# A fifth buffer for q and k rows, and a new written-out order for all engines, in a one-core transformer block

## The chip, the cores and the metric

The kernel runs on one core of one Trainium2 chip. A core has five engines that are used here, each with its own queue of instructions: PE (TensorE: matrix products, into eight PSUM banks), DVE (VectorE), ACT (ScalarE), POOL (GpSimd) and SP (SyncE, which only issues transfers here). Transfers (DMAs) are issued from the queues of SP and POOL, and one from ACT's. The metric is the device time of one execution in microseconds (us); lower is better.

## The reference, cut to what matters

The input `x` is 2048 tokens of 448 features, in bf16. Everything starts from the layer-normalised `xn`:

```python
x = A_x
xn = _layernorm(x, axis=-1)
s = _A_ref(xn, A_wqkv, A_wo)                          # attention: 16 heads of 28, each token sees
                                                      # itself and 7 earlier ones, two apart
g = _silu(_B_ref(xn, B_w1, B_b1, B_w2, B_b2))         # MLP: gelu(xn @ w1 + b1) @ w2 + b2, 448 -> 1792 -> 448
return x + s * g
```

`_A_ref` makes q, k and v from `xn @ wqkv`, takes a softmax over the eight logits of a token and a head, weighs v with it and multiplies by `wo`.

## The kernel before, in words

**Tiles.** The tokens are reordered so that even ones come before odd ones; a window two apart then has neighbouring rows. They make 16 token tiles of 128 rows (t = 0 to 15) and four chunks of 512 (c = 0 to 3). The work of one token tile is: statistics (`stats`, L327), `rstd` (`rstds`, L338), normalisation (`norm`, L361), a transpose to `xnT` (on PE for tiles 0 to 3, by a DMA that SP issues, `dma_T` L274, for the others), the products for its q rows, k rows and v rows (`qk_rows` L448, `vproj` L471), and the copies of these out of PSUM. q and k rows go to a buffer `qk_tok` (L456 to L464), from which one DMA per tile writes them transposed to `qkT`; a buffer may be written again only when that DMA has landed (the third dependency in L461). Before the change there are four such buffers, and tile t uses buffer t mod 4. v rows are copied by DMAs that POOL issues (`values`, L485) into 128-row windows for the attention.

**MLP.** `ff1` (L506) makes 14 tiles of the hidden layer for each chunk, ACT applies the gelu; `ff2` (L530) makes one token tile of the result in two halves of seven products each; a token tile's result passes DVE, ACT (a tanh, or a silu for the last chunk) and DVE.

**Attention.** Nine blocks of 228 or 224 tokens (b = 0 to 8). `scores` (L660) is 64 small products into four banks, ACT takes the exponential, DVE multiplies by a mask, `values_sum` (L665) is 64 small products into two banks, DVE divides (`output_of`, L631: transpose, reciprocal, transpose, multiply), `final` (L673) multiplies by `wo`, then by the MLP's result, adds x and stores.

**Pairs and hops.** The products with 448 rows of contraction (q, k, v, ff1) run in pairs (`pair`, L401): a first part A of eight products, where the two jobs of a pair use the two halves of PE's rows at the same time, and a second part B of six with the halves exchanged. Between A and B stands a hop (L412): a nop on POOL or SP that waits for the end of A, and for which B waits. A hop stands in that engine's queue like any instruction: what is ahead of it in the queue delays B.

**The order.** There are 938 tasks, numbered in the order in which the code adds them. The string `ORDER` (L17) lists all of them; a word is an engine's letter (P = PE, V = DVE, A = ACT, G = POOL, S = SP, D = a transfer's landing) and a task's number. Each engine's instructions are issued in just this order, and PSUM banks and ring buffers are taken and given back in it (`emit`, L94). Tasks that may run on two engines (copies out of PSUM, hops) run on the one whose letter stands there.

The words that are spoken of below:

| words | task |
|---|---|
| P132 to P138 | first products of tiles 0 and 1, six batches and a last one |
| P149, P151; P128, P129 | q, k of tile 2, parts A and B; PE transposes of tile 3 |
| P190, V191 | transpose of the bias b1 on PE (L768), its copy |
| P308 A, P310 B; P313, P315; P318, P320; P323, P325; P333, P335; P338, P340 | ff1 of chunk 0, hidden tiles 0-1; 2-3; 4-5; 6-7; 10-11; 12-13 |
| P227, P215, P234, P208 | part A of q, k of tiles 6, 5, 7, 4 (P229, P217, P236, P210: part B) |
| A218, V219 or A219; A237, A238; A211, A212 | copies of q and k rows of tile 5; tile 7; tile 4 |
| S141, S146, S154, S161 | DMA that turns q and k rows of tile 0, 1, 2, 3 |
| S202, S206, S198, S194 | DMA that turns xn of tile 6, 7, 5, 4 |
| G99, G98, G307, G298 | rstd of tiles 6-7; 4-5; 12-15; 8-11 (L349) |
| G100, G102, G104 | building the three masks (L726) |
| G309, G314, G334, G529, G539 | hops before P310, P315, P335, P530, P540 |
| P691, P772 | scores of block 0; values of block 4 |
| G399, G403, G405 | POOL's DMAs of v rows of tile 8 for block 4 |

Of the kernel before, what the change touches and what calls it, by code (L numbers as in the profile page):

```python
# [11 lines left out]
ACT = mybir.ActivationFunctionType  # L12
# [3 lines left out]

ORDER = """  # L17
D0 V1 G17 S34 D35 A36 D37 V15 V16 P2 V22 S38 D39 V23 G50 V24 G51 D52 V25 V26 P3 V27 V28 S44 D45 V29 V30 G31 V18 V19
G32 P4 V20 G33 V21 S40 D41 P5 A53 S42 D43 P6 G100 S46 D47 P7 V60 P8 S48 D49 P9 V61 S76 D77 G102 V64 A62 P10 S78 D79
V63 P11 P12 V106 P13 S80 D81 P14 V107 P108 V65 S82 D83 P109 G104 A66 V110 S86 D87 V67 A111 D112 P132 V113 S88 D89  # L20
V114 P115 P116 S90 D91 V68 P136 A117 A118 D119 P133 V69 V72 A70 P134 V71 V120 P135 V121 V73 V101 P122 A74 A54 P123
V103 P137 V75 V124 D125 P138 V126 V127 P149 V105 A139 V140 A144 P128 G150 P129 V145 S141 D142 P151 A130 D131 V143
P190 A152 P308 V153 G168 D169 A148 V94 G170 D171 P313 S154 D155 G309 V95 G172 D173 V84 P310 G314 G174 D175 V85 P315
V191 V96 G178 D179 A311 P156 G176 D177 V97 V92 A312 G99 P163 V93 A316 P318 A317 G157 G164 V200 G98 P158 V201 V204
S202 D203 V205 P165 A159 V160 G319 P320 A166 V167 S206 D207 P323 G180 D181 A321 V196 V197 G182 D183 V192 P328 A322
S198 D199 V193 G324 G184 D185 P325 G329 G186 D187 S194 S146 D147 D195 P330 G188 D189 A326 P227 G246 D247 A327 S161
D162 P234 A331 G228 G252 D253 P229 A332 G235 G280 D281 S272 D273 P236 S274 D275 V231 A230 P215 S276 D277 P208 G216
S232 D233 P217 G209 P210 A218 V219 S278 D279 P333 A211 V212 S220 D221 P338 G334 P335 G339 A237 V238 P340 A336 S213
D214 P528 A337 P533 A341 G529 A342 P530 G534 P535 A531 V296 P538 A532 V297 V290 S239 D240 P543 A536 G539 V291 V294
A537 P540 V295 G544 V305 P545 A541 V306 V299 P548 A542 V300 V303 P553 A546 G549 V304 V301 A547 P550 G554 V302 V292  # L30
G307 P555 A551 V293 P558 A552 P222 A556 V431 G559 G298 V432 G223 P560 V427 A557 S433 D434 V419 P241 A561 G242 P224
A562 A225 A55 G248 D249 G282 D283 V428 V420 G284 D285 P243 A245 G286 D287 G288 D289 V423 G250 D251 V424 P691 A694
S429 D430 V226 V355 V356 S425 D426 S421 D422 V244 P568 P569 P508 A692 V570 G254 D255 A571 V572 V693 P513 P514 A698
V699 P727 P518 V515 V343 V351 V344 A696 G256 D257 P509 A516 V517 A732 G258 D259 V695 A728 V697 P700 G260 D261 S357
V347 D358 G262 D263 V348 A734 V735 V352 S345 D346 V510 A511 A730 V701 S349 D350 G264 D265 V702 V703 V705 P519 V520
V706 V707 S353 D354 V708 P523 V704 G266 D267 P524 P709 A712 V713 A716 V512 A714 V715 V731 G268 D269 V525 P359 S360
A710 P366 S367 P361 A362 P368 A370 P385 V363 G270 D271 V717 S386 P378 G379 P387 P380 S364 D365 V369 V711 P718 S371
D372 A388 G397 D398 P853 A389 V382 P573 A381 S383 D384 V719 P745 V723 V724 S390 D391 V733 V854 A748 A752 V855 V725
A750 P563 P574 A521 V720 V749 V721 V722 P564 V522 A746 V726 P863 V729 S856 D857 A526 P858 P736 V565 P454 V527 V864
G401 D402 V859 V860 G455 V741 P461 V575 P456 A457 V865 V737 G462 A458 V747 P449 V742 V743 V738 S866 D867 S459 D460  # L40
V744 P463 A464 A465 P468 S466 D467 G450 P451 V453 P442 G469 V751 P470 A471 V739 P435 S443 P444 V740 A446 A445 A566
G436 P437 A439 V753 V472 P754 V438 S440 D441 P868 P763 V452 V759 A766 V760 V869 P873 V870 V761 V567 V874 A768 A770
V762 A764 S447 D448 P578 P579 V580 A576 V577 V755 P781 A786 P373 A782 A788 V756 S871 D872 S861 D862 P583 S584 G374
P375 V376 G407 D408 P585 A784 A56 A377 P588 A581 S589 V757 G409 D410 V758 G411 D412 V767 V765 P593 P392 S594 A587
P590 P595 A586 G415 D416 V769 G399 D400 V771 V875 S393 A591 G403 D404 G473 P603 S876 D877 P394 S604 A597 P608 V395
A596 G405 D406 G413 D414 G417 D418 V789 G474 D475 P605 V787 A396 P772 G476 D477 G478 D479 G480 D481 A592 G482 D483
A606 V785 G484 D485 G486 D487 P598 V582 A607 S609 V773 V774 G488 D489 P613 V775 G490 D491 V783 S599 P600 G492 D493
V776 G494 D495 A602 A601 S614 P615 A616 P610 V777 V778 V779 V780 A612 P790 V795 P618 V791 A617 V796 A611 A57 P799
A800 V797 V798 G496 D497 P888 V889 P619 V620 P878 A804 V890 P883 A802 G498 D499 P817 S891 D892 V879 A818 V803 G500
D501 A621 A806 V880 V807 A822 P628 V805 G502 D503 V801 V884 P623 V792 V793 A820 V622 G504 D505 A824 P629 V630 V794  # L50
P808 V809 V810 V811 P624 G506 D507 P835 P893 A842 A840 V813 P633 P634 A838 V812 A836 A58 V635 A636 P648 V894 V895
S896 D897 P638 V814 V637 A631 P643 G639 S881 D882 V815 V816 V821 P640 A642 A641 V843 V625 V885 S649 P650 S644 A652
P645 P653 V823 A626 V819 A647 V841 P658 A646 S659 G654 V632 A651 P655 A657 A656 V825 V627 P660 S886 D887 A661 P826
V831 V837 P668 V832 V833 A662 G669 P663 G664 P670 V834 P665 A667 A671 A666 V839 P844 V849 P903 V904 V905 S906 D907
P908 V909 V910 V850 A672 A59 V827 P681 S911 D912 P682 V828 V829 V830 P673 V845 V851 P898 P674 P913 V899 V675 V900
A676 V846 V683 V847 P918 V848 A684 V852 V914 V915 S916 D917 P677 P678 V679 A680 V919 S901 D902 V920 S921 D922 P923
V924 P685 P686 V925 S926 D927 A687 P928 V929 V930 P688 P689 P933 A690 V934 V935 S931 D932 S936 D937
"""


# [58 lines left out]
def kernel(  # L119
# [13 lines left out]
    P = 128  # L133
    S, D, H, DH, F = A_x.shape[1], 448, 16, 28, 1792
# [16 lines left out]
    for v in range(9):  # L151
        n = NW - 1 if v == 4 else NW
        q = 4 * NW * v - 4 * (v > 4)
# [17 lines left out]
    def sb(name, shape, dt=BF16):  # L171
        return const.tile(shape, dt, name=name)
# [27 lines left out]
    def ring(name, n, shape, dt=BF16):  # L200
        return _Pool([sb(f"{name}{i}", shape, dt) for i in range(n)])
# [13 lines left out]
    p_g.bufs = p_g.bufs + late_g  # L215
    p_h = ring("h", 28, [P, CH])
    p_v = ring("v", 6, [P, H, 32])
    qk_tok = [sb(f"qk_tok{i}", [P, 2, H, 32]) for i in range(4)]
    p_b = _Pool([psum.tile([P, 512], F32, name=f"bank{i}") for i in range(8)])

    plan = _Plan()

    def buf(pool, owner, i=0):
        return pool.bufs[owner.slots[pool][i]]

    def copy(e, o, i):
        if e == "ACT":
            nc.scalar.copy(o, i)  # L228
        else:
            nc.vector.tensor_copy(o, i)  # L230


    def memset(eng, ap, v):
        def fn(_):
            getattr(nc, eng).memset(ap, v)
        return fn

    warm = p_h.bufs[-1]
    t_on = plan.add("DMA", lambda _: None, ())
# [12 lines left out]
                                base=0, pattern=[[-1, P]], channel_multiplier=1)  # L252
    t_ident = plan.add("POOL", mk_ident, [t_on])

    t_qz = [plan.add("DVE", memset("vector", q[:, :, :, DH:], 0.0), [t_on]) for q in qk_tok]
    t_vw = [plan.add("DVE", memset("vector", v[:, :, DH:], 1.0), [t_on]) for v in v_tok[:9]]
    t_row0 = plan.add("POOL", memset("gpsimd", row0[:], 0.0), [t_on])
    t_row0 = plan.add("POOL", memset("gpsimd", row0[:1, :], 1.0), [t_row0])
# [132 lines left out]
    def half_rows(half):  # L391
        return slice(64 * half, 64 * half + 64) if half < 2 else slice(0, P)
# [53 lines left out]
    t_row, t_qk = [[] for _ in range(NT)], {}  # L446

    def qk_rows(t, which):  # L448
        cs = slice(t * P, (t + 1) * P)

        def part(ps, kt, half, start, stop):
            r = half_rows(half)
            w = w_in[r, kt, which * D:(which + 1) * D] if kt < 3 else w_in3[r, 0, :]
            return nc.tensor.matmul(ps[:, :D], xnT[r, kt, cs], w, start=start, stop=stop)  # L454

        def evac(a, own, i):  # L456
            b = qk_tok[t % len(qk_tok)]

            def fn(k):
                copy(k.on, b[:, which, :, :DH], buf(p_b, own, i)[:, :D].rearrange("p (h c) -> p h c", h=H))  # L460
            t_row[t].append(plan.add(("ACT", "DVE"), fn, [a, t_qz[t % len(qk_tok)], t_qk.get(t - len(qk_tok))], give=((p_b, own, i),)))  # L461
            if len(t_row[t]) == 2:
                t_qk[t] = dma_T(qkT[:, :, :, cs].rearrange("p w g c -> p (w g) c"), lambda: b[:].rearrange("p w h c -> p (w h c)"),
                                t_row[t], None)  # L464
        return _Job(D, part, [t_xT[t]] + t_w[0] + t_w[1] + t_w[2], evac, (), t_w[3])
# [368 lines left out]
```

## Time and profile before

| what | value |
|---|---|
| three runs | 155.38, 156.09 and 156.47 us; median 156.09 |
| the profiled execution: its own time | 155.29 us |
| its span, first to last instruction | 153.6 us, so 1.69 us lie around it |
| PE busy | 148.3 us (97% of the span), 2200 products |
| DVE / ACT / POOL busy | 111.9 / 85.1 / 43.6 us (73 / 55 / 28%) |
| share of the chain that ended last | PE 83%, DMA 5%, DVE 4%, POOL 3%, SP's queue 2% |
| DMA that turns q and k rows, issue to landing | 3.1 / 4.9 / 8.1 us (least, median, most of 16) |
| the same for xn | median 3.3 us (12 of them) |

A profile line such as "L546 PE MATMUL ... x238 | 45.1, 342" means: 238 instructions of line 546, 45.1 us busy in all, 342 ns for one. Products are pipelined, so one lasts longer than the distance to the next; the cost of a product on PE's path is that distance. In the chain by time a line gives the start, the length and the work, in us. In the list of waits a line gives the waiting engine and what it waited for, then the total, the number of times and the longest.

### The profile page before, as it was taken

To read this page: it belongs to the slowest core of one execution; us is meant where nothing else is said; L and a number is where in the kernel's file an instruction comes from. 1 tells how busy PE (TensorE), PEld (TensorE's weight loads), DVE (VectorE), ACT (ScalarE), POOL (GpSimd) and SP (SyncE) were. 2 spreads that over 40 slices of the span, in tenths; PEclk is the share of its full clock that TensorE was granted. 3 is DMA by queue.
4 is the path that set the end of the run, shared out by engine and by line. 5 is a ranking of instruction groups with operands and counts; after the bars stand their busy time and mean duration, and the time that the engine had idled before them with its cause. 6 is when DMAs were issued, how large, how long until landed. Compare 5 with 4: busy or idle time off the path is not lost.

```text
span 153.6 us, 5265 instructions
## 1 busy us (share of the span) xinstructions
PE 148.3 (97%) x2200; PEld 80.9 (53%) x2200; DVE 111.9 (73%) x280; ACT 85.1 (55%) x158; POOL 43.6 (28%) x95
## 2 busy tenths in 40 slices
PE   6899999999999999999999999999999999999992
PEld 2444445578775555555554554455455444455561
DVE  4998541459262699969897997389859497797973
ACT  3474665368886350737043759739670859580320
POOL 7854865000359116020000004499500000000000
PEclk9999999999999999999999999999999999999999
DMA  5999998999987635079217370323300010010022
GB/s 149 326 276 324 126 187 168 226 343 257 165 112 150 111 73 103 4 147 131 63 34 137 74 132 19 98 71 86 81 30 4 4 60 30 4 47 17 0 89 65
DMA packets 33576, 17.36 MB, mean 113 GB/s; under 512 B 25203, under 2 KB 32387, under 8 KB 33552
## 3 DMA queue, kind: packets, MB, share of 16 engines
q1 hardware_dynamic: 31472, 14.03, 44.5%
q0 software_dynamic: 1936, 2.88, 7.9%
q8 instruction: 17, 0.28, 0.8%
q10 hardware_dynamic: 144, 0.11, 0.2%
q14 instruction: 7, 0.06, 0.1%
HBM read 7.06 MB, written 1.84 MB: 58 GB/s over the span
## 4 chain that ended last, share of the span: by engine, by line
PE 83%; DMA 5%; DVE 4%; POOL 3%; SPq 2%; issue 1%; ACT 1%; POOLq 0%; ACTq 0%
PE bank L546 28%; PE bank L512 22%; PE bank L454 10%; PE bank L681 8%; PE bank L477 6%; PE bank L627 4%; PE bank L595 4%; DMA qkT<-qk_tok 3%; POOL v L270 2%; DMA x_sb<-in_A_x_dram 2%; SPq L276 2%; DVE xn L363 1%; DVE st L329 1%; PE bank L378 1%; DVE xn L368 0%
## 5 line engine op out<-in xcount | busy, mean ns | idle before, releaser
L546 PE MATMUL bank<-w,h 128*128 128x448 bf16 (+2 forms) x238 | 45.1, 342 | 0.0
L512 PE MATMUL bank<-xnT,w 64*128 64x512 bf16 x392 | 44.7, 376 | 0.3 <-ACT qk_tok L228 0.3
L270 POOL DMA_DIRECT2D v<-v_tok x52 | 27.3, 532 | 48.4 <-DVE v_tok L230 27.1
L516 ACT ACTIVATE h<-bank,b 128x512 bf16<-128x512 f32 x56 | 34.2, 692 | 12.3 <-PE bank L512 12.2
L512 PEld LDWEIGHTS <-w 64*128 64x128 bf16 x392 | 23.1, 94 | 18.7 <-issue 1.0
L546 PEld LDWEIGHTS <-h 128*128 128x128 bf16 x238 | 22.1, 98 | 18.9
L605 ACT ACTIVATE E<-bank 128x456 bf16<-128x456 f32 (+1 forms) x36 | 17.2, 551 | 14.8 <-PE bank L595 14.8
L454 PE MATMUL bank<-w_in,xnT 64*128 64x448 bf16 (+1 forms) x212 | 24.0, 350 | 0.2 <-DVE xnT L230 0.2
L228 ACT CAST qk_tok<-bank 128x448 bf16<-128x448 f32 x20 | 9.9, 534 | 13.7 <-PE bank L454 9.8
L454 PEld LDWEIGHTS <-xnT 64*128 64x128 bf16 (+1 forms) x212 | 10.4, 94 | 10.1 <-issue 0.4
L561 DVE TENSOR_TENSOR y<-bank,b 128x448 f32<-128x448 f32 x15 | 9.2, 612 | 7.6 <-PE bank L546 7.6
L681 PE MATMUL bank<-wo,oT 128*128 128x448 bf16 (+2 forms) x68 | 14.3, 342 | 0.0
L637 DVE STREAM_TRANSPOSE dt<-bank 128x480 f32<-128x480 f32 (+1 forms) x18 | 11.8, 662 | 2.9 <-PE bank L627 1.7
L477 PE MATMUL bank<-w_in,xnT 64*128 64x448 bf16 (+1 forms) x106 | 13.8, 349 | 0.0
L230 DVE CAST qk_tok<-bank 128x448 bf16<-128x448 f32 x12 | 7.2, 620 | 8.7 <-PE bank L454 5.2
L646 DVE STREAM_TRANSPOSE dt<-rd 128x480 f32<-128x480 f32 (+1 forms) x18 | 12.0, 668 | 0.3
L329 DVE BATCH_NORM_STATS2 st<-x_sb 128x6 f32<-128x448 bf16 x16 | 9.7, 603 | 3.2 <-DMA x_sb<-in_A_x_dram 3.2
L651 DVE TENSOR_TENSOR oT<-bank,dt 128x456 bf16<-128x456 f32 (+1 forms) x18 | 11.1, 625 | 0.3
L611 DVE TENSOR_TENSOR E<-E,m_gen 128x456 bf16<-128x456 bf16 x28 | 10.0, 379 | 1.8 <-ACT E L605 1.8
L573 ACT ACTIVATE t<-y 128x448 f32<-128x448 f32 x12 | 6.9, 581 | 6.2 <-DVE y L561 6.2
L363 DVE TENSOR_SCALAR xn<-x_sb,mv,rstd 128x448 bf16<-128x448 bf16 x16 | 6.1, 394 | 4.7 <-POOL rstd L351 4.5
L230 DVE CAST v_tok<-bank 128x448 bf16<-128x448 f32 x9 | 5.6, 619 | 5.1 <-PE bank L477 5.1
(62 smaller groups left out, 120.6 us busy)
## 6 DMA issues: line engine op xcount, KB each, us to landing
out_dram<-o SPq DMA_DIRECT2D x15, 112.0 KB, 1.8
w<-in_B_w_dram SPq DMA_DIRECT2D x2, 784.0 KB, 7.4
w<-in_B_w_dram SPq DMA_DIRECT2D x2, 672.0 KB, 7.6
x_sb<-in_A_x_dram SPq DMA_DIRECT2D x3, 448.0 KB, 6.2
v<-v_tok POOLq DMA_DIRECT2D x20, 64.0 KB, 2.9
w_in<-in_A_wqkv_dram SPq DMA_DIRECT2D x3, 336.0 KB, 4.0
w<-in_B_w_dram SPq DMA_DIRECT2D x4, 112.0 KB, 7.1
wo<-in_A_wo_dram POOLq DMA_DIRECT2D x4, 98.0 KB, 3.8
```

Source lines behind the costliest of these rows:

```text
L230: nc.vector.tensor_copy(o, i)
L270: nc.gpsimd.dma_start(dst(k), src())
L329: nc.vector.bn_stats(out=buf(p_st, k)[:], in_=x_sb[:, t, :])
L454: return nc.tensor.matmul(ps[:, :D], xnT[r, kt, cs], w, start=start, stop=stop)
L477: return nc.tensor.matmul(ps[:, :D], xnT[r, kt, k0:k0 + P], w, start=start, stop=stop)
L512: return nc.tensor.matmul(ps[:], w1[r, kt, ms], xnT[r, kt, cs], start=start, stop=stop)
L516: nc.scalar.activation(buf(p_h, own, i)[:], buf(p_b, own, i)[:], ACT.Gelu_apprx_tanh, bias=b1[:, mt:mt + 1])
L546: nc.tensor.matmul(ps[:, :n], buf(*h_at[(c, mt)])[:, j * P:(j + 1) * P], w2[:, mt, cs], start=(mt == 0 and not biased), stop=(mt == NMT - 1))
L605: nc.scalar.activation(buf(p_E, k)[:, :n], buf(p_b, a, hl)[:, :n], ACT.Exp, scale=SCALE)
L637: nc.vector.transpose(buf(p_dt, k)[:, :32 * m], buf(p_b, po, i)[:, :32 * m])
L646: nc.vector.transpose(buf(p_dt, d)[:, :32 * m].rearrange("p (b c) -> p b c", c=32), buf(p_rd, r)[:, :m].unsqueeze(2).to_broadcast((P, m, 32)))
L681: nc.tensor.matmul(ps[:, :n], oT[:, kt, t * P:(t + 1) * P], wo[:, kt, cs], start=(kt == 0), stop=(kt == KT - 1))
```

## The change

It adds one buffer for q and k rows. Buffers 3 and 4 are halves of one tile, `qk_pair`, whose unused columns are cleared by one memset instead of two. Which tile uses which buffer is now a list, and the task that a copy waits for is the transfer of the last tile that used the same buffer. The string `ORDER` is replaced as a whole: the tasks are the same 938, and their number on PE is the same.

By task number, 15 copies out of PSUM go from DVE to ACT (v0, k1, v3, k6, k5, k7, k4, v5, v6, k8, k10, v12, v13, q12, v10) and eight from ACT to DVE (two of xnT, then v7, q8, q11, q13, v14, v11); eight hops go from POOL to SP and four from SP to POOL. The code, and those lines of `ORDER` that hold the words above, cut:

```diff
 ORDER = """
-G32 P4 V20 G33 V21 S40 D41 P5 A53 S42 D43 P6 G100 S46 D47 P7 V60 P8 S48 D49 P9 V61 S76 D77 G102 V64 A62 P10 S78 D79
-V63 P11 P12 V106 P13 S80 D81 P14 V107 P108 V65 S82 D83 P109 G104 A66 V110 S86 D87 V67 A111 D112 P132 V113 S88 D89
-V114 P115 P116 S90 D91 V68 P136 A117 A118 D119 P133 V69 V72 A70 P134 V71 V120 P135 V121 V73 V101 P122 A74 A54 P123
-V103 P137 V75 V124 D125 P138 V126 V127 P149 V105 A139 V140 A144 P128 G150 P129 V145 S141 D142 P151 A130 D131 V143
-P190 A152 P308 V153 G168 D169 A148 V94 G170 D171 P313 S154 D155 G309 V95 G172 D173 V84 P310 G314 G174 D175 V85 P315
...
-S198 D199 V193 G324 G184 D185 P325 G329 G186 D187 S194 S146 D147 D195 P330 G188 D189 A326 P227 G246 D247 A327 S161
-D162 P234 A331 G228 G252 D253 P229 A332 G235 G280 D281 S272 D273 P236 S274 D275 V231 A230 P215 S276 D277 P208 G216
-S232 D233 P217 G209 P210 A218 V219 S278 D279 P333 A211 V212 S220 D221 P338 G334 P335 G339 A237 V238 P340 A336 S213
...
-P590 P595 A586 G415 D416 V769 G399 D400 V771 V875 S393 A591 G403 D404 G473 P603 S876 D877 P394 S604 A597 P608 V395
-A596 G405 D406 G413 D414 G417 D418 V789 G474 D475 P605 V787 A396 P772 G476 D477 G478 D479 G480 D481 A592 G482 D483
...
+G32 P4 V20 G33 V21 S40 D41 P5 A53 S42 D43 P6 G100 S46 D47 P7 V60 P8 S48 D49 P9 V61 S76 D77 V64 A62 P10 S78 D79 V63
+P11 P12 V106 P13 S80 D81 P14 V107 P108 V65 P109 A66 V110 P132 V67 V113 V114 P115 V117 A111 V68 D112 P136 P116 A118
+P133 V69 A70 V71 S82 D83 V120 V121 S86 D87 P190 G102 V72 V73 A74 D119 P137 S88 D89 S90 D91 V191 P134 P122 P123 V124
+P135 P138 A139 D125 P149 G150 A143 G168 D169 V75 V126 V127 V140 P128 G170 D171 P129 V130 A148 A54 G172 D173 P151
+V153 D131 P318 G319 A145 P163 A152 G174 D175 V101 P320 S141 D142 A144 A321 A322 G178 D179 P156 S154 D155 V84 G176
+D177 P313 V96 G164 P165 V85 P333 V97 V94 V95 V92 A167 G99 V200 V204 G314 P315 A166 G334 V205 P335 A316 V201 S202
+D203 G157 V93 G98 S206 D207 P158 V196 V197 G180 D181 S198 D199 G182 D183 V192 V193 A336 P308 S194 D195 V160 A159
+G309 A317 S146 D147 S161 D162 G184 D185 P323 G324 G186 D187 G188 D189 A337 P310 A311 S272 D273 V290 P325 P328 A326
...
+A231 A332 S276 D277 G216 P217 V301 A219 P338 G339 P548 P340 G549 P550 P234 G235 A341 V103 A218 A551 P208 A342 G104
+P236 A237 A238 A552 V105 V296 P538 V304 P543 G539 G544 S232 D233 V300 P540 A542 G209 P210 P553 G554 A211 P545 S278
+D279 A212 P533 G534 S220 D221 V302 S213 D214 A546 A547 P555 V305 V306 G307 V423 V419 V427 A541 A557 V428 P528 G529
...
+P392 G415 D416 G405 D406 V582 V875 P595 V785 V771 A587 G393 P603 P590 G403 D404 A596 V769 A591 P394 S876 D877 G473
+V396 A592 A395 G413 D414 V765 G417 D418 S604 G474 D475 G476 D477 G478 D479 P605 A607 P608 A576 P613 A597 A606 V789
+P772 V777 S614 S609 P610 G480 D481 G482 D483 A611 A612 G484 D485 G486 D487 P598 S599 P615 P600 A617 V778 V774
...
-    qk_tok = [sb(f"qk_tok{i}", [P, 2, H, 32]) for i in range(4)]
+    qk_pair = sb("qk_pair", [P, 2, 2, H, 32])
+    qk_tok = [sb(f"qk_tok{i}", [P, 2, H, 32]) for i in range(3)] + [qk_pair[:, i] for i in range(2)]
+    qk_at = [0, 1, 2, 3, 4, 0, 2, 1, 3, 4, 0, 2, 1, 3, 4, 0]
...
-    t_qz = [plan.add("DVE", memset("vector", q[:, :, :, DH:], 0.0), [t_on]) for q in qk_tok]
+    t_qz = [plan.add("DVE", memset("vector", q[:, :, :, DH:], 0.0), [t_on]) for q in qk_tok[:3]]
+    t_qz += [plan.add("DVE", memset("vector", qk_pair[:, :, :, :, DH:], 0.0), [t_on])] * 2
...
-            b = qk_tok[t % len(qk_tok)]
+            b = qk_tok[qk_at[t]]
+            free = t_qk.get(max([u for u in range(t) if qk_at[u] == qk_at[t]], default=None))
...
-            t_row[t].append(plan.add(("ACT", "DVE"), fn, [a, t_qz[t % len(qk_tok)], t_qk.get(t - len(qk_tok))], give=((p_b, own, i),)))
+            t_row[t].append(plan.add(("ACT", "DVE"), fn, [a, t_qz[qk_at[t]], free], give=((p_b, own, i),)))
```

More of the change, by code (lines that the diff above doesn't have):

```diff
@@ L23 @@
-P190 A152 P308 V153 G168 D169 A148 V94 G170 D171 P313 S154 D155 G309 V95 G172 D173 V84 P310 G314 G174 D175 V85 P315
-V191 V96 G178 D179 A311 P156 G176 D177 V97 V92 A312 G99 P163 V93 A316 P318 A317 G157 G164 V200 G98 P158 V201 V204
-S202 D203 V205 P165 A159 V160 G319 P320 A166 V167 S206 D207 P323 G180 D181 A321 V196 V197 G182 D183 V192 P328 A322
-S198 D199 V193 G324 G184 D185 P325 G329 G186 D187 S194 S146 D147 D195 P330 G188 D189 A326 P227 G246 D247 A327 S161
-D162 P234 A331 G228 G252 D253 P229 A332 G235 G280 D281 S272 D273 P236 S274 D275 V231 A230 P215 S276 D277 P208 G216
@@ L28 @@
-S232 D233 P217 G209 P210 A218 V219 S278 D279 P333 A211 V212 S220 D221 P338 G334 P335 G339 A237 V238 P340 A336 S213
[L29 to L42, printed above, removed]
@@ L43 @@
-V762 A764 S447 D448 P578 P579 V580 A576 V577 V755 P781 A786 P373 A782 A788 V756 S871 D872 S861 D862 P583 S584 G374
-P375 V376 G407 D408 P585 A784 A56 A377 P588 A581 S589 V757 G409 D410 V758 G411 D412 V767 V765 P593 P392 S594 A587
-P590 P595 A586 G415 D416 V769 G399 D400 V771 V875 S393 A591 G403 D404 G473 P603 S876 D877 P394 S604 A597 P608 V395
-A596 G405 D406 G413 D414 G417 D418 V789 G474 D475 P605 V787 A396 P772 G476 D477 G478 D479 G480 D481 A592 G482 D483
-A606 V785 G484 D485 G486 D487 P598 V582 A607 S609 V773 V774 G488 D489 P613 V775 G490 D491 V783 S599 P600 G492 D493
@@ L48 @@
[L48 to L57, printed above, removed]
+G32 P4 V20 G33 V21 S40 D41 P5 A53 S42 D43 P6 G100 S46 D47 P7 V60 P8 S48 D49 P9 V61 S76 D77 V64 A62 P10 S78 D79 V63
@@ new lines @@
+D203 G157 V93 G98 S206 D207 P158 V196 V197 G180 D181 S198 D199 G182 D183 V192 V193 A336 P308 S194 D195 V160 A159
+G309 A317 S146 D147 S161 D162 G184 D185 P323 G324 G186 D187 G188 D189 A337 P310 A311 S272 D273 V290 P325 P328 A326
+G246 D247 V291 A327 P227 G329 P330 V294 V295 A331 S274 D275 V299 P215 G252 D253 G280 D281 V303 A312 G228 P229 A230
+A231 A332 S276 D277 G216 P217 V301 A219 P338 G339 P548 P340 G549 P550 P234 G235 A341 V103 A218 A551 P208 A342 G104
+P236 A237 A238 A552 V105 V296 P538 V304 P543 G539 G544 S232 D233 V300 P540 A542 G209 P210 P553 G554 A211 P545 S278
@@ new lines @@
+D279 A212 P533 G534 S220 D221 V302 S213 D214 A546 A547 P555 V305 V306 G307 V423 V419 V427 A541 A557 V428 P528 G529
+P558 G559 A556 P535 A537 V431 P530 A532 P560 S239 D240 V432 V297 P222 A561 A531 A536 S433 D434 V292 G223 P241 V424
+S429 D430 A562 S425 D426 P224 G242 P243 V293 G298 A225 A55 P691 A692 V420 G248 D249 A698 V355 S421 D422 V356 S357
+D358 A694 G282 D283 G284 D285 P508 P509 P568 P569 A226 A696 P513 P518 V695 V693 V697 P514 V510 G286 D287 V343 G288
+D289 V699 G250 D251 V351 V352 A511 A244 V245 G254 D255 V512 V570 V347 V348 V344 A571 V572 P700 V701 P519 V515 A516
@@ new lines @@
+P727 A728 S345 D346 V520 G256 D257 A521 G258 D259 V702 G260 D261 V705 A730 V706 A734 V707 G262 D263 V703 S349 D350
+P523 V704 A732 V708 P524 P709 G264 D265 S353 D354 V517 A712 P359 A716 G266 D267 S360 P378 V713 V525 V522 A526 P361
+A714 S379 A363 P380 A381 P366 S367 V362 S364 D365 V729 V717 G268 D269 A710 V711 P385 P368 A370 V715 V369 A382 S371
+D372 S383 G270 D271 D384 V735 G386 P387 V388 P718 A389 V719 V720 V721 S390 D391 V722 P853 P745 V854 P573 V855 A748
+V723 V724 A752 V527 V731 V725 V726 A746 V733 P858 P563 V859 P564 V565 P574 V575 P863 A566 V567 S856 D857 P736 G397
@@ new lines @@
+D398 V864 V865 P454 P461 G401 D402 V747 A750 S455 P456 P442 V737 A457 A458 G462 V741 V742 P463 P449 V743 V744 G443
+V738 V739 S866 D867 A465 P444 S459 D460 V751 A464 A446 P435 V740 G450 S466 D467 V749 S436 V445 P451 A452 A453 P468
+P437 V860 G469 V753 P470 V472 P754 P868 A438 A439 V471 S440 D441 V869 P763 S447 D448 A766 A770 V870 S871 D872 V755
+A768 V756 P873 V874 A764 V757 V758 P578 P579 V580 V759 P781 A784 V767 V760 A786 S861 D862 P373 A581 A782 P583 S374
+P375 G584 A788 A377 A56 V376 G407 D408 G409 D410 G411 D412 P585 V761 P588 P593 S594 S589 V762 G399 D400 V787 A586
@@ new lines @@
+P392 G415 D416 G405 D406 V582 V875 P595 V785 V771 A587 G393 P603 P590 G403 D404 A596 V769 A591 P394 S876 D877 G473
+V396 A592 A395 G413 D414 V765 G417 D418 S604 G474 D475 G476 D477 G478 D479 P605 A607 P608 A576 P613 A597 A606 V789
+P772 V777 S614 S609 P610 G480 D481 G482 D483 A611 A612 G484 D485 G486 D487 V773 P598 S599 P615 P600 A617 V778 V774
+V783 P790 V775 V776 P878 V779 A602 V791 V780 G490 D491 A601 G488 D489 G494 D495 A616 A57 V879 V795 G492 D493 V792
+V793 V796 P888 P799 A800 V889 A806 A802 A804 V577 P618 P619 V794 V890 V807 P883 V884 V805 P817 A824 V620 A820 P628
@@ new lines @@
+P835 A838 V801 A818 V803 V797 V798 P629 P808 V813 A836 P893 G496 D497 G498 D499 V630 P633 V814 V815 A621 A840 P623
+V816 V825 V885 V622 A631 V632 P624 P634 S891 D892 A842 G500 D501 A822 A58 P643 P648 S644 V894 V895 S896 D897 P645
+V635 P663 V841 A636 V843 V880 S881 D882 G502 D503 G504 D505 S649 V809 V625 V810 V811 V812 V823 A646 V837 A626 A647
+V839 P650 S664 V819 P665 P638 A667 A666 V821 P653 A652 S639 A651 P640 S654 G506 D507 V637 P655 A657 A656 V627 S886
+D887 A641 P826 V827 P668 S669 V828 V831 P658 S659 V829 V830 P670 A671 A642 P660 A661 V832 A672 A662 A59 V833 V834
@@ L58 @@
+P844 P903 V904 V905 S906 D907 P898 V899 P908 V909 V910 S911 D912 P918 P913 V845 V846 V847 V900 S901 D902 V848 V849
+V850 V851 V852 P673 P674 V675 P681 P682 P923 P677 P678 P685 V683 A676 V914 V915 S916 D917 A684 V924 V925 S926 D927
+V679 A680 P686 V919 V920 A687 S921 D922 P928 V929 V930 P688 P689 A690 S931 D932 P933 V934 V935 S936 D937
 """
```

## Prediction

> **What bounds the kernel now.** I read the page's busy times and slices first, then the list of waits, then the chain in order of time, and last the timelines of single engines around the places found.
>
> ```profile
> PE 148.3 (97%) x2200; PEld 80.9 (53%) x2200; DVE 111.9 (73%) x280; ACT 85.1 (55%) x158; POOL 43.6 (28%) x95
> PE   6899999999999999999999999999999999999992
> PEclk9999999999999999999999999999999999999999
> ```
>
> TensorE works in every slice but the first two and the last, at full clock. So no engine beside it can be relieved for a gain; only what PE loses between its products counts. The waits that reach it are few:
>
> ```profile
> ACT qk_tok L228 <- DMA qkT<-qk_tok: 3.4, 2, 3.2
> DVE qk_tok L230 <- DMA qkT<-qk_tok: 3.2, 1, 3.2
> PE bank L512 <- ACT qk_tok L228: 0.3, 1, 0.3
> ```
>
> ACT and DVE both stand still for 3.2 us for the landing of a q/k transpose, and PE then waits for ACT to free a bank. The chain in time shows the same place, and a second one:
>
> ```profile
> 23.79 5.02 DMA qkT<-qk_tok
> 28.80 0.02 issue
> 28.82 0.02 ACTq L228
> 28.84 0.04 issue
> 28.88 0.54 ACT qk_tok L228
> 29.42 0.04 issue
> 29.46 12.38 PE bank L512 x112
> ...
> 91.48 0.86 PE bank L512 x8
> ...
> 100.27 0.96 PE bank L627 x64
> ...
> 105.01 0.61 PE bank L627 x64
> ```
>
> S146 (tile 1) is issued at 23.79 and lands 5.02 us later; A218, the copy of tile 5, waits for it, because four buffers make tile 5 take tile 1's; P338 waits for A218's bank. Eight L512 products cost 0.86 us. On PE's timeline the eight of P333 take 1.34:
>
> ```profile
> 28.12 1.03 PE L512 MATMUL bank<-xnT,w 64*128 64x512 bf16 x8
> 29.46 1.88 PE L512 MATMUL bank<-xnT,w 64*128 64x512 bf16 x15 [0.32 <-ACT qk_tok L228]
> ```
>
> So 0.48 us is lost there. The values of block 4 (100.27) take 0.96 against 0.61 for others: 0.35 lost. Their last v rows are the ones that POOL issues here, behind copies of v:
>
> ```profile
> 94.77 3.10 POOL L270 DMA_DIRECT2D v<-v_tok  x6 [0.36 <-ACT v_tok L228]
> ```
>
> G403 and G405 start at 96.84 and 97.34 and land at 100.43 and 100.59, after P772 began at 100.20.
>
> **The change, part by part.** PE's products are the same, so I lay the new PE order end to end with the row costs of before (0.86 for an L512 part A, 0.65 B; 0.76 and 0.57 for q/k/v; 1.32 for half an ff2; 0.76 final; 0.7 scores or values), and ask at each task whether its inputs and bank can be there.
>
> *The first 12 us.* P132 still starts at 5.99, after the copy of tile 0. Before, P137 to P151 fill 9.35 to 12.45, 3.10 us for 2.71 of work: four pauses of 0.1; then P190 0.16, and ff1 starts at 12.61. After, P190 moves ahead: 5.99 plus 4.64 of products ends P138 at 10.63, A 0.76 and transposes 0.23 reach 11.62, a pause of 0.1 for the hop, B 0.57: ff1 at 12.35, when the first half of w1 has landed (12.30). Gain 0.25. Bounds: all pauses stay, 0; none stays, 0.35. The copy V117 is now ahead of tile 2's statistics on DVE (0.3 us plus its wait), so xn of tile 2 comes at 9.2 instead of 8.8; P122 needs it at 9.26. Cover is thin but there.
>
> *The fifth buffer.* Tile 4 gets a fresh buffer, tile 5 that of tile 0 (landed 17.03), tile 6 that of tile 2 (21.29); only tile 7 waits for S146. Its copies A237 and A238 follow P236, which ends at 31.9 in the new order. S146 should go out at 22.9 (below). With its 5.0 us it lands at 27.9; with the longest of 16 rows at 31.0:
>
> ```profile
> DMA to landing us min/median/max: 3.1/4.9/8.1
> ```
>
> So 0.48 goes, and nothing takes its place unless a transpose needs 9 us. The memset of the pair is one instead of two, twice as wide: 0.11 to 0.22 us, on a DVE that idles 1.23 us until x lands at 3.38. It costs nothing.
>
> [...]
>
> *xn of tiles 4 to 7.* Three statistics of 0.76 us from the landing of x at 13.35 end at 15.7; G99 then runs 15.7 to 16.8 (16.80 to 17.91 before); the four transposes and S146 behind them go out about 0.9 us earlier. Even at the old landings (22.01, 24.45, 25.84 for tiles 6, 5, 4) their first users start later: P227 23.5, P215 24.9, P548 27.7.
>
> *Copies moved to ACT.* Fifteen copies come (0.53 each), eight go. From 26.9 to 44.2 ACT has 17 gelus, 0.57 apart, and seven copies 0.44 apart: 12.8 us in 17.3. That holds, but in-order: the last four gelus follow P560 (41.6) and end at 44.0, and the scores P691 need their banks at 44.2. Bounds here: 0 to 0.7 (one gelu late); I take 0, by the sum.
>
> *POOL's queue.* G99, G98, G104 and G307 now stand ahead of hops. G314 after G99: 16.8, P315 needs it at 17.7. G309 after G98 and two issues: 20.1 to 20.6, needed at 21.3. G539 after G104 (2.19 us after P234's end at 30.6): 32.9, needed at 33.7. G529 after G307: x of tiles 12 to 15 landed at 33.60, DVE then needs 4.0 us to the last statistic, G307 1.4: 39.0, needed at 40.3. All covered; the last hangs on a transfer.
>
> *v rows of block 4.* The hop G584 no longer waits behind anything; the copy of v rows of tile 8 ends at 92.4, and six issues of 0.53 put G403 last at 95.6. With the latencies of these three rows (3.3 to 3.9) it lands by 99.5; P772 starts at 100.0. Gain 0.35. Bounds: gain 0.35; with the longest v row in the list of issues (6.6 us) a loss of 2.2. I take the nearest rows, the same transfers.
>
> *SP's queue.* S436 stands behind two transposes (1.23 and 1.26 us) and passes about 1 us ahead of its need; S649 behind a store that waits for DVE, 1 us ahead too. Nothing.
>
> *The end.* The last products and what follows them are the same: 3.09 us from P933's end to the span's.
>
> Sum: 0.25 + 0.48 + 0.35 = 1.08. Span 152.5, with the 1.69 around it 154.2 against 155.29. That execution was 0.80 below the median of the runs shown, so for a median I carry the same 0.80: **155.0 us**, 0.7% below 156.09. About 1% is what a measurement of this kernel can tell from no change.
>
> **Rivals.** *More is gained.* The 0.80 us between that execution and the median may itself be later landings; if the new slack hides them as well, the time is 154.2. For it: both waits that cost PE most hang on transfers. Against: one profile cannot tell whether the 0.80 lies in the span.
>
> *The waits only move.* Where I count 0 with 0.1 to 0.3 us to spare (xn of tile 2, P691's banks, P378's bank after the first exponential of block 1, the gelus ahead of P603 and P598), each may cost what the old places cost, 0.1 to 0.48. Five at 0.2 eat 1.0: 156.0. For it: before has four such pauses by 12.5. Against: they are counted with measured rows.
>
> *Slower.* G307 is ahead of the hop G529, and G307 waits for x of tiles 12 to 15. From a landing 1.2 us after the old 33.60, each us goes straight to P530. The forecast gain is used up at 35.9. The two halves of w2 on the same queue landed at 35.63 and 40.51; halfway, 38.1, costs 3.3 us: 158.3. For it: that queue is full from 26 to 45, single issues take up to 4.44 us. Against: the loads stand in the same order and start earlier.
>
> **How the numbers follow.** Forecast 0.50 (own range 154.4 to 155.6), more gained 0.22, only moved 0.18, slower 0.10. Faster by over 1% (under 154.53) takes the second and 0.08 of the first: 0.30. Slower by over 1% (above 157.65): 0.10. Within: 0.60. The range 154.0 to 156.6 leaves out the slow rival and about 0.1 of tails.
>
> **What would show it.** After should have no wait of ACT or DVE qk_tok on DMA qkT near 28 us; ff1 should start near 12.35; block 4's values should take 0.61; PE should end near 149.4. Wrong would be: a PE wait for POOL's hops at L512 between 15 and 41, scores of block 0 waiting for ACT h, or PE's last product after 150.5.

## The result and the profile after

The changed kernel takes 154.94 us (median of 11 runs, 154.47 to 155.44) beside 156.14 us of the kernel before (median of 11, 155.38 to 156.91). The ratio is 0.9938, with a 95% interval from 0.9917 to 0.9959: 0.6% faster, which is 1.0 us by the ratio and 1.2 us by the medians. No change, a ratio of 1, lies outside the interval, but the change is smaller than the 1% that the prediction took for what a measurement of this kernel can tell. The forecast was 155.0.

The two profiled executions differ by much less: 155.29 before, 155.02 after, spans 153.6 and 153.3. That is already a hint that the first profile of before was not a typical one. The page of the changed kernel begins like this:

```profile
PE 148.6 (97%) x2200; PEld 78.6 (51%) x2200; DVE 107.3 (70%) x273; ACT 89.0 (58%) x165; POOL 43.0 (28%) x95
...
PE   6999999999999999999999999999999999999991
...
PEclk9999999999999999999999999999999999999999
```

TensorE is still the bound. Work has gone from DVE (111.9 to 107.3 us) to ACT (85.1 to 89.0), and neither is near full. In the list of waits (engine, what it waited for, us in total, times, longest) the lines that showed ACT and DVE waiting for a q/k transpose are gone. What is left for the q/k copies is mostly waiting for TensorE itself:

```profile
ACT qk_pair L230 <- PE bank L457: 3.6, 3, 2.3
...
ACT qk_tok L230 <- PE bank L457: 0.6, 2, 0.4
```

In the chain in time (start, us, what) the place of the old 0.48 us pause at 29 us is one unbroken run of products, and the values of block 4, which took 0.96, take 0.60:

```profile
25.75 1.89 PE bank L457 x20
27.64 3.02 PE bank L516 x28
30.66 2.08 PE bank L457 x22
...
100.99 0.60 PE bank L631 x64
```

From the start of ff1 to the end of the last product, TensorE needs 136.94 us after and needed 137.90 before: 0.96 us less, which is the two places and 0.1 at the scores of block 0. But ff1 starts at 13.10 instead of 12.61, 0.49 later. Half of the gain is hidden there, and the first 13 us on TensorE's timeline show where. Before:

```profile
5.99 0.55 PE L454 MATMUL bank<-w_in,xnT 128*128 128x448 bf16 x2 [0.23 <-DVE xnT L230]
6.38 0.35 PE L477 MATMUL bank<-w_in,xnT 128*128 128x448 bf16 x1
```

And after:

```profile
6.00 0.93 PE L457 MATMUL bank<-w_in,xnT 128*128 128x448 bf16 x2 [0.17 <-DVE xnT L232]
6.72 0.58 PE L481 MATMUL bank<-w_in,xnT 128*128 128x448 bf16 x1
```

The same three products (P132) start at the same moment, but they take 1.09 us after and 0.59 before: in this execution TensorE was still at about half rate (373 ns from one product to the next, against 190 later). This is no part of the change: in the second profile of the changed kernel (below) they take 0.64 us, and they take 1.09 also in the old order with its four buffers, in the run below that moves only the v rows.

### The profile page after: what moved, and what is told of

It reads as the page before. It is cut to its first block, busy times and chain, and to the rows that moved or that the text cites. A ratio compares the mean times of both kernels' runs of the same rounds, so it can differ in the third digit from the quotient of the medians.

```text
span 153.3 us, 5268 instructions
## 1 busy us (share of the span) xinstructions
PE 148.6 (97%) x2200; PEld 78.6 (51%) x2200; DVE 107.3 (70%) x273; ACT 89.0 (58%) x165; POOL 43.0 (28%) x95
## 4 chain that ended last, share of the span: by engine, by line
PE 97%; DVE 1%; issue 0%; ACT 0%
PE bank L550 28%; PE bank L516 28%; PE bank L457 14%; PE bank L685 8%; PE bank L481 7%; PE bank L599 4%; PE bank L631 4%; PE bank L245 3%; PE bank L381 1%; DVE xnT L232 0%; DVE sg L691 0%; ACT w_in L572 0%; DVE h L237 0%; DVE o L699 0%; PE bank L548 0%
## 5 line engine op out<-in xcount | busy, mean ns | idle before, releaser
L520 ACT ACTIVATE h<-bank,b 128x512 bf16<-128x512 f32 x56 | 35.4, 689 | 11.2 <-PE bank L516 11.2
L516 PEld LDWEIGHTS <-w 64*128 64x128 bf16 x392 | 20.4, 94 | 20.9 <-issue 0.8
L457 PE MATMUL bank<-w_in,xnT 64*128 64x448 bf16 (+1 forms) x212 | 24.8, 352 | 0.2 <-DVE xnT L232 0.2
L609 ACT ACTIVATE E<-bank 128x456 bf16<-128x456 f32 (+1 forms) x36 | 17.8, 549 | 10.0 <-PE bank L599 9.3
L457 PEld LDWEIGHTS <-xnT 64*128 64x128 bf16 (+1 forms) x212 | 10.9, 94 | 9.5 <-DVE xnT L232 0.4
L481 PE MATMUL bank<-w_in,xnT 64*128 64x448 bf16 (+1 forms) x106 | 13.7, 352 | 0.0
L230 ACT CAST qk_tok<-bank 128x448 bf16<-128x448 f32 x17 | 8.4, 536 | 1.6 <-PE bank L457 0.6
L685 PEld LDWEIGHTS <-oT 128*128 128x128 bf16 x68 | 6.0, 98 | 4.9
L481 PEld LDWEIGHTS <-xnT 64*128 64x128 bf16 (+1 forms) x106 | 5.8, 95 | 5.1 <-issue 0.2
```

The lines of the kernel that those rows point to most:

```text
L481: return nc.tensor.matmul(ps[:, :D], xnT[r, kt, k0:k0 + P], w, start=start, stop=stop)
L516: return nc.tensor.matmul(ps[:], w1[r, kt, ms], xnT[r, kt, cs], start=start, stop=stop)
L520: nc.scalar.activation(buf(p_h, own, i)[:], buf(p_b, own, i)[:], ACT.Gelu_apprx_tanh, bias=b1[:, mt:mt + 1])
L609: nc.scalar.activation(buf(p_E, k)[:, :n], buf(p_b, a, hl)[:, :n], ACT.Exp, scale=SCALE)
L685: nc.tensor.matmul(ps[:, :n], oT[:, kt, t * P:(t + 1) * P], wo[:, kt, cs], start=(kt == 0), stop=(kt == KT - 1))
```

## The experiments

The theory: TensorE lost time at fixed places that wait for transfers (the transpose of tile 1, the v rows of block 4), and the change removes these. The rivals: the new order as a whole does it and the buffer does nothing; or the gain lies where the first profile could not show it. Kernels are compared with runs of the kernel before on the same chip. "Old order" and "new order" are the ORDER strings of the two kernels.

**Both kernels again, unchanged.**

> The kernel before, unchanged, for a second profile. Theory A (the time spreads because TensorE leaves its half rate at a moment that differs between executions, and because transfers land at differing times): the losses at the fixed places stay, about 0.4 us before block 0's products of tile 5 (P338) and about 0.35 at the values of block 4, while the first 12 us differ: with full rate only at about 7 us instead of 4.5, ff1 starts up to 0.5 us later than 12.61 and the span is up to 0.9 us longer than 153.6. Rival (the 0.8 us between the first profiled execution and the median lie outside the span): span 153.6 within 0.1.

> The changed kernel, unchanged, for a second profile. Theory A: no pause of TensorE over 0.15 us behind the start of ff1, whatever the landings; what differs from the first profile lies ahead of ff1's start (13.10 there): between 12.3 and 13.2. From there to the end of the last product 136.9 us within 0.2. Rival (landings move the pauses about): a pause of 0.2 to 0.5 somewhere behind 13 us.

The kernel before took 155.02 us with a span of 153.3: at the start it was 0.26 slower than in its first profile (ff1 at 12.87), behind it 0.53 faster (137.37 us to the end of the products). The wait for the transpose is still in the list, but half as long, and does not reach TensorE, because this time S146 landed at 27.89 instead of 28.80:

```profile
ACT qk_tok L228 <- DMA qkT<-qk_tok: 1.7, 1, 1.7
```

The values of block 4 wait as before; in its chain all but one of their 64 products take 0.93:

```profile
100.05 0.93 PE bank L627 x63
```

So Theory A was right about the values and the start, and wrong about P338, which lost nothing. The span is 0.3 us below the first one's: outside the 0.1 that the rival allowed, and not longer, as Theory A had it, because what was gained behind the start was more than what was lost at it. The changed kernel took 154.71, with ff1 at 12.80 and 136.95 us from there to the end: the same as in its first profile to 0.01. So in these two profiles of the new order nothing varies behind 13 us, and in the two of the old order something does.

**The fifth buffer alone, and the order alone.** Against the kernel before, the first takes the buffers of the change and leaves ORDER as it was:

```
-    qk_tok = [sb(f"qk_tok{i}", [P, 2, H, 32]) for i in range(4)]
+    qk_pair = sb("qk_pair", [P, 2, 2, H, 32])
+    qk_tok = [sb(f"qk_tok{i}", [P, 2, H, 32]) for i in range(3)] + [qk_pair[:, i] for i in range(2)]
+    qk_at = [0, 1, 2, 3, 4, 0, 2, 1, 3, 4, 0, 2, 1, 3, 4, 0]
```

The second leaves the four buffers (tile t takes t % 4) and takes the new ORDER:

```
-D0 V1 G17 S34 ... (the old ORDER)
+D0 V1 G17 S34 ... (the new ORDER)
```

> The order of before with the five buffers of the changed kernel. Theory A: the 3.4 and 3.2 us that ACT and DVE wait for a q/k transpose near 26 to 29 us are gone, P338 starts on time, 0.48 us less: 155.66 for a median of 156.14. Rival (another wait takes its place, or the transposes then collide): 156.1 or more.

> The new order of all engines with the four buffers of before. Theory A (the fifth buffer is worth what the wait cost): the copies of tile 5 wait for tile 1's transpose again and 0.3 to 0.5 us of the gain is lost: 155.3 to 155.5. Rival B (the new order puts the copies of tile 5 at 28.6 and 30.6 us, behind the landing of 27.75 seen in the changed kernel, so that the fifth buffer has nothing left to do): 154.9 to 155.0, with no wait of ACT or DVE for that transpose over 0.3 us.

The buffer alone: 155.65 beside 155.79, ratio 0.9974 (0.9947 to 1.0001), with 137.07 us from ff1 to the end and no pause at P338, though S146 landed only at 30.58. By time alone this is too little to be told from nothing. The order alone: 154.48 beside 155.79, ratio 0.9911 (0.9879 to 0.9942), with 137.00 us. Rival B is right about the second: with four buffers the new order is no slower than with five (its time came out 0.4 us below what Rival B had). ACT's timeline in that kernel shows why:

```profile
28.02 0.54 ACT L228 CAST qk_tok<-bank 128x448 bf16<-128x448 f32 x1
...
30.07 0.52 ACT L228 CAST qk_tok<-bank 128x448 bf16<-128x448 f32 x1
```

The copies of tile 5 stand at 28.02 and 30.07, and S146 had landed at 27.33. The cover is 0.7 us, and it held in the profile. Part of it is that the transpose itself is quicker in the new order: 3.64, 3.92 and 4.07 us from issue to landing (after, its repeat, order alone) against 5.02, 3.82 and 5.84 in the old order (before, its repeat, buffer alone). The later profiles in which it was not delayed agree: 3.76 and 3.77 in the new order, 4.99, 5.20 and 5.07 in the old one. Why it is quicker, the runs do not show.

**One transfer made late.** To see what the buffer does then, S146 is put behind the transpose of tile 3 and two loads of x, in the kernel before, in the changed one, and in the new order with four buffers:

```
-S146 D147 S161 D162 ... S272 D273 ... S274 D275
+S161 D162 ... S272 D273 ... S274 D275 S146 D147
```

> The kernel before with one transfer made late: the transpose of q/k tile 1 goes out behind the one of tile 3 and two loads of x instead of ahead of them, about 3 us later, so that it lands at about 31.3 us instead of 28.8. Theory A (TensorE waits for this landing through the copy of tile 5, and one for one): P338 starts at about 31.9 instead of 28.98, 2.4 us more than before: 158.2, between 157.2 and 159.2. Rival (the wait is hidden by other work of TensorE): 156.3 or less.

> The changed kernel with the same transfer made late in the same way. Theory A (with five buffers only tile 7 needs that buffer, from 32.8 us on): no wait, 154.9 within 0.3. Rival (later landings move the wait to tile 7): 155.5 or more, with ACT waiting for that transpose near 33 us.

> The new order with four buffers and the same transfer made late. Theory A (the fifth buffer is an insurance: the new order alone covers landings to about 28.6 us, the buffer those to 32.8): ACT waits 2 to 3 us ahead of the copy of k of tile 5, and the time is 1.5 to 2.7 us over the same kernel without the delay: 156.0 to 157.2. Rival (the order alone covers it): 154.5 to 154.9, as without the delay.

| kernel | S146 issued, landed | lost by TensorE near 30 to 41 us | time |
|---|---|---|---|
| before, late | 27.43, 35.71 | 7.8 | 163.25, ratio 1.046 (1.039 to 1.053) |
| new order, four buffers, late | 26.51, 34.53 | 6.9 | 161.48, ratio 1.030 (1.022 to 1.038) |
| changed, late | 26.46, 34.70 | 2.1 | 157.98, ratio 1.011 (1.004 to 1.019) |

All three were late by more than I expected: behind the loads the transpose took 8.0 to 8.3 us instead of 3.6 to 5.8. So the times that I had put down were too low in each, by 3 to 5 us, but where TensorE waits is plain. The chain of the kernel before with the delay runs from the transpose straight into the products:

```profile
27.43 8.28 DMA qkT<-qk_tok
...
35.78 0.54 ACT qk_tok L228
...
36.37 13.83 PE bank L512 x112
```

With four buffers in the new order, ACT stops ahead of k of tile 5, and behind it TensorE; this is ACT's timeline:

```profile
34.61 0.53 ACT L228 CAST qk_tok<-bank 128x448 bf16<-128x448 f32 x1 [6.16 <-DMA qkT<-qk_tok]
```

With five, ACT works on until tile 7's copies, and stops there; its timeline again:

```profile
34.80 0.97 ACT L230 CAST qk_tok<-bank 128x448 bf16<-128x448 f32 x2 [2.79 <-DMA qkT<-qk_tok]
```

So the rival to the late changed kernel came true (the wait moves to tile 7), at a landing of 34.7.

Not all that is lost is waiting. In the late kernel before, and in the new order with four buffers, the row of the granted clock drops at and behind the wait (each in 40 slices of 4.0 us):

```profile
PEclk9999999956999999999999999999999999999999
PEclk9999999975999999999999999999999999999999
```

When TensorE goes on there, the clock is at 0.50 and the products take about twice their time for 3 to 5 us: P338 1.66 us instead of 0.86, P208 1.69 instead of 0.76. Of the 7.8 us lost by the kernel before, 6.3 are the wait and 1.5 the rate; of the 6.9 us with four buffers, 4.2 and 2.7. In the profile of the changed kernel the clock stays at 1.00, and the 2.1 us are all wait. Its four runs fall into two groups: 157.03 and 157.04 us at a mean granted clock of 1.000 (one of them is the profiled one), and 158.91 and 159.06 at 0.989 and 0.986.

The buffer moves the point from which a late transpose costs something from about 28 to about 32 us, and was worth about 3 us here: 161.48 - 157.98 = 3.5 by the medians of four runs each, 2.9 by the two ratios. By the profiles 2.1 us of it is a shorter wait and the rest the rate behind it. In the undisturbed profiles of the new order S146 landed between 27.33 and 28.10: the buffer had nothing to do. It is insurance, not gain.

**The v rows of block 4 alone, then both repairs.** The kernel before with the rows that come from tile 8 issued first; then the same together with the five buffers:

```
-V376 G407 D408 ... G409 D410 ... G411 D412 ... G415 D416 ... G399 D400 ... G403 D404 ... G405 D406
+V376 G399 D400 G403 D404 G405 D406 G407 D408 ... G409 D410 ... G411 D412 ... G415 D416
```

> The kernel before with one edit: the three v rows of block 4 from tile 8 are issued ahead of those of block 5 instead of behind them, so that they go out at 93.9 to 95.5 us and land by 99.5. Theory A (the values of block 4 wait for these landings): P772 takes 0.61 us instead of 0.96 and the time falls by 0.35: 155.5 to 155.8 beside 155.8 to 156.1. Rival (block 5's rows, now last, are late at their values): 104.94 is where they are needed, and no change is left.

> The order of before with the five buffers and with block 4's v rows issued first: the two repairs without the rest of the new order. Theory A (these two places are where the gain lies): as fast as the changed kernel, ratio 0.991 to 0.995 to before. Rival (other pauses that the new order removes weigh as much): 0.996 or more, and its profile shows where TensorE still pauses.

The rows alone: 155.75 beside 156.05, ratio 0.998 (0.9948 to 1.0012): too small to be told from nothing by time, but the chain shows the repair. The values of block 4 take 0.60, while the other place still costs 0.43:

```profile
101.14 0.60 PE bank L627 x64
```

Both repairs: 155.62 beside 156.04, ratio 0.9969 (0.9939 to 0.9999). From ff1 to the end this kernel needs 136.98 us, as little as the changed one. So behind 13 us these two places are the whole of it; and yet its median is 0.7 us over that of the changed kernel, and its ratio is in the range of the rival and not in that of Theory A (the intervals of the two ratios overlap). The other pauses that the rival had in mind are not there behind 13 us. Two things are left, the start and the tail.

The start: over the profiles, ff1 begins at 12.61, 12.87, 13.57, 13.56, 13.03 and 13.66 in the old order (mean 13.22) and at 13.10, 12.80, 12.53, 12.79, 12.84, 13.53 and 12.67 in the new one (mean 12.89; the last two are of the last experiment below): 0.33 us, with a standard error of 0.2, so that these profiles alone don't show it beyond doubt. In the late run of the kernel before, TensorE's timeline shows a reason:

```profile
7.71 0.35 PE L477 MATMUL bank<-w_in,xnT 128*128 128x448 bf16 x1
9.04 0.54 PE L454 MATMUL bank<-w_in,xnT 128*128 128x448 bf16 x2 [0.98 <-DMA w_in<-in_A_wqkv_dram]
```

P134 waits for the second row block of w_in. It landed at 9.00 here, and at 7.90 in the first profile of before, where P134 wanted it at 7.99: just in time. Over 14 profiles, which issue it alike at 2.65 to 2.68, it lands between 7.55 and 9.53 us (12 of them behind 7.99). The new order asks for it later, because P137 and P190 stand ahead of P134. Where P134 could have started (0.57 us behind the start of the group ahead of it) is 7.9 to 8.5 us in the six profiles of the old order, and it waited 0.44 us there in the mean; it is 8.6 to 9.2 in the seven of the new order, with a mean wait of 0.08.

**That one move alone.**

```
-P133 V69 V72 A70 P134 V71 V120 P135 V121 V73 V101 P122 A74 A54 P123 V103 P137
+P133 V69 V72 A70 P137 P134 V71 V120 P135 V121 V73 V101 P122 A74 A54 P123 V103
```

> The kernel before with one product group moved: P137 (the third k range of w_in for tile 1) stands ahead of P134 and P135 (the second k range), as in the new order, so that P134 asks for the second row block of w_in 0.57 us later, at 8.56 instead of 7.99. In the 13 profiles so far, which all issue these loads alike, that block landed at 7.55 to 9.53 us, median 8.37. Theory A (this landing, late in most executions, is the part of the gain that the first profile of before could not show): the mean loss at P134, worked out from the 13 landings, falls from 0.53 us to 0.20, so 0.3 us less: 155.7 for 156.0, and a wait of P134 in the profile only if the block lands behind 8.56. Rival (the landing is no part of it; P137 then waits for its own block): same time as before within 0.1 and a pause at P137.

Median 155.52 beside 156.11, ratio 0.9988 (0.9955 to 1.0021): inconclusive in time. The timeline is clear. The block landed at 8.68; the old order would have stood at P134 from 8.33; here P137 fills 8.33 to 8.90, and P134 runs on without a wait:

```profile
8.33 0.54 PE L454 MATMUL bank<-w_in,xnT 128*128 128x448 bf16 x2
...
8.90 0.54 PE L454 MATMUL bank<-w_in,xnT 128*128 128x448 bf16 x2
```

The mean loss worked out from the first 13 landings is 0.55 us for an asking time of 7.99 and 0.21 for 8.56, which is where the order alone has it (8.57). So the move explains the earlier start by the landings; its time of its own is not shown.

**The price of the slower rival.** The load of x tiles 12 to 15 (S274) goes behind the second half of w2 (S278); then, in addition, G307 behind the four hops that follow it on POOL:

```
-S274 D275 S276 D277 ... S278 D279 ... V306 G307 ... G529 ... G559 ... G223 ... G242
+S276 D277 ... S278 D279 S274 D275 ... V306 G307 ... G529 ... G559 ... G223 ... G242
```

```
-S274 D275 S276 D277 ... S278 D279 ... V306 G307 ... G529 ... G559 ... G223 ... G242
+S276 D277 ... S278 D279 S274 D275 ... V306 ... G529 ... G559 ... G223 ... G242 G307
```

The statistics and normalisations that need what is moved follow it.

> The changed kernel with the load of x tiles 12 to 15 put behind the second half of w2 on its queue, so that it lands at about 40 us instead of 34.5. This tries the price of the slower rival of the prediction. If the rule on record holds (each us of landing beyond a small cover goes to P530 by way of G307 and the hop behind it): four statistics of 0.65 us from 40 us, G307 to 44.1, P530 at 44.6 instead of 40.9: about 3.5 us more, 158.4, between 157.4 and 159.4. Against it (TensorE has other work there or the load is not late): below 156.

> As the kernel with the late load of x, but with the reciprocal roots of tiles 12 to 15 put behind the four hops of POOL that they stood ahead of. If the place in POOL's queue is what costs: 154.9 to 155.4, with no wait of TensorE at 41 us. If the late statistics cost by themselves, through DVE or the transposes behind them: 156 or more.

The late load costs 159.28 (ratio 1.0194, 1.0145 to 1.0243), 4.3 us over the changed kernel. The chain has it in one piece:

```profile
33.40 6.83 DMA x_sb<-in_A_x_dram
...
40.25 1.68 DVE st L332 x3
...
43.07 0.31 POOL sd L353
...
43.49 2.35 PE bank L516 x12
```

The path is the one on record, but the sizes are not. The hop passes at 43.42, when G307's first instruction has ended, and TensorE goes on at 43.49; G307's second instruction runs from 43.46 to 44.50. The prediction and the expectation had counted this second one, 1.0 us, as ahead of the hop. So TensorE waited 2.2 us and not 3.5. Another 1.7 us are its rate behind the wait: the granted clock is 0.50 from 44 to 46 us, and P222 takes 1.49 us instead of 0.76. That the time is within the expected bounds is in part luck.

With G307 behind the hops it is still 158.32 (1.0133, 1.0079 to 1.0187). The wait at 41 us is gone, but then DVE waits 3.9 us at a stretch for transposes of xn that free its buffers, with the additions behind ff2 queued behind, and TensorE loses 2.3 us at the scores of block 2. The expectation that put the whole price on POOL's queue is wrong: the place there is worth 1.0 of the 4.3 us, as far as medians of four runs can tell, and the late statistics the other 3.4.

## Why the prediction was right, and where it was not

The time (154.94 for 155.0), the sign, and the size (1.0 to 1.2 us for 1.08) came out. The steps behind them did less well:

- **From ff1 to the last product: right.** The record has ff1 at 12.35 and PE's end at 149.4, 137.05 us; measured 136.94 and 136.95. None of the thin covers failed: the four gelus end at 44.83, and P691 starts at 44.95; G307 ends at 39.95, and P530 starts at 40.90. "The waits only move" did not come true in these two profiles. Nor did the slower rival: x of tiles 12 to 15 landed at 34.52, within the 34.8 that the prediction left for it.
- **The values of block 4, 0.35: right.** The record has G403 out at 95.6, landed by 99.5, and P772 at 100.0, with ff1 at 12.35. In the profile ff1 is 0.75 us later. Counted from ff1, G403 went out 0.45 us later than on record (96.80), landed 0.2 earlier (100.08), and P772 started 0.2 later (100.92). The cover was 0.8 us, and 0.55 in the repeat.
- **The fifth buffer, 0.48: the wait goes, but not by the buffer.** "So 0.48 goes" named the cause that the change's words name. The order alone removes it, and the buffer alone does too; together the second has nothing to do. Of the 3.2 us that ACT stood still, only the last 1.1 can be the landing's: P217, the products that the copy needs as well, ended at 27.72. Also 0.48 is one draw: four profiles in the old order with four buffers and no added delay lost 0.48, 0, 0.43 and 0.53 there, 0.36 in the mean. S146 went out at 24.11, not at 22.9.
- **The first 12 us, 0.25: the mechanism failed.** I took the four pauses of 0.1 for waits that the move of P190 and earlier hops would shorten. They are still there in the new order (0.09, 0.10, 0.09 and 0.18 us in the changed kernel, where one kind of product follows another), and where P190 stood, the pause ahead of ff1 is now 0.18 instead of 0.11: ff1 starts 0.15 us behind the end of the copy of tile 3, which it needs. Net of that, order alone starts ff1 at 12.53 for 12.61. What gains there as far as the landings show it, P137 ahead of P134, I costed at nothing, since the profile showed the weights in time, by 0.09 us. Over the profiles the start of ff1 is 0.33 us earlier. That 0.25 is near this is luck.
- **The tail, "the same": wrong by 0.2.** From TensorE's end to the span's end it is 3.07 before, 3.05 with the order alone, 3.26 and 3.25 in the changed kernel, and 3.47 and 3.50 with five buffers in the old order.
- **The 0.80 us carried to the median: right in the end by luck.** It was added as one constant to both kernels, and it is not one: the median lies 0.85 us over the profiled execution before, and 0.08 under it after. Part of what the first execution of before had by chance is its early ff1 (12.61 beside a mean of 13.22), and the sum had a gain at the start for another reason. The executions of the kernel before scatter more (standard deviation 0.64 us over 78 runs) than those of the changed one (0.31 over 11). That fits landings which reach TensorE in the old order; no run shows the cause of the scatter by itself. Span and time differ by about 1.7 us in every run of both kernels, so the scatter lies in the span.

The sum as measured: 0.33 (start) + 0.36 (tile 1's transpose) + 0.35 (mean at the values, from 0.35, 0.47, 0.53 and 0.09 in the four undelayed profiles of the old order in which the rows had not moved) + 0.1 (scores of block 0) - 0.2 (tail) = 0.9 us, beside the 0.97 of the ratio (0.64 to 1.30). The start alone is uncertain by 0.2. The first profile of before showed 0.48 and 0.35 of it, and nothing of the start.

The new order with four buffers has the lowest median, 154.48, and the short tail. It was not run beside the changed kernel, and the intervals of the two ratios overlap, so it is not shown to be faster; it would also lose the insurance.

## What to carry to other kernels

A profile is one execution. Where a transfer lands within a few tenths of the moment when it is wanted (here 7.90 for 7.99), write down its scatter from all the profiles at hand and cost the mean of the lateness, not the one draw. When a change does two things for one wait, run each alone before naming the cause. And to price an insurance, make the transfer late: about 3 us showed at once what 0.3% in undisturbed runs could not. Then part the wait from the rate of TensorE behind it, by the clock and by the time of one product.

## What the runs showed of the hardware

- **TensorE's half rate at the start ends at differing moments.** In the first profile of before the 128-column warm-up products take 57 ns each from 4.48 us on; in that of the changed kernel they take 107, and the 448-column products of P132 still 373 at 6.0 to 7.1 us, against 190 later. The rows PEclk read full speed in both. The moments at which the products become quick lie some 2.6 us apart in these two traces; what sets them, the runs do not show. The slower rate cost up to 0.5 us, and not by kernel: over the 14 profiles P132 took 0.58 to 1.09 us, and 1.09 in one profile of each order.
- **Behind a wait TensorE can fall back to half rate.** In the profiles, after standing 6.17 us (kernel before, late), 4.03 (new order with four buffers, late) and 1.98 (late load of x) it had a granted clock of 0.50 for 3 to 5 us and took about twice the time for a product. After 1.90 us (changed kernel, late) and 1.72 (late load of x, G307 behind the hops) it kept 1.00.
- **The same load, issued at 2.65 to 2.68 us in every kernel, landed between 7.55 and 9.53 us.** That scatter of 2 us is larger than the whole effect of the change.
- **The tail.** With five buffers and the old order the last store takes 0.4 us longer to land behind its issue (1.5 against 1.1); in the changed kernel the store is as quick as before, but DVE's last drain ends 3.05 us behind TensorE's end instead of 2.57, after those of the other engines, and the span ends 0.2 us later. The first shows in both kernels of that kind, the second in each of the five profiles with the five buffers and the new order. Why, the runs do not show; it stays open.
